# Fixed buffers for the z2 tiles of a gMLP kernel: which buffer each of the last two tiles takes

## The chip, the cores and the metric

The kernel runs on one core of a Trainium2 chip. The metric is the time of one execution in device microseconds; a kernel's time is the median of several runs. Five engines work beside each other and wait for one another through semaphores: PE (TensorE, matmuls), ACT (ScalarE), DVE (VectorE), POOL (GpSimd) and SP (SyncE). Each runs its own instructions in order. DMAs are issued from the queues of SP, ACT and POOL.

## The reference

One block: a layer norm with modulation, a long convolution (an S4 state space model), and then a gMLP, which is where the change lies:

```python
z = gelu(einsum("bsd,df->bsf", x, w_in))        # s = 2048 rows, f = 4608
z1 = z[..., :2304]
z2 = layernorm(z[..., 2304:], axis=-1)
g = einsum("ts,bsf->btf", w_sp, z2) + b_sp[None, :, None]
out = einsum("bsf,fd->bsd", z1 * g, w_out)
```

The layer norm of z2 needs a whole row of 2304 values, and g sums over all 2048 rows, so every row of z2 must be finished before the first g is complete.

## The kernel before

The first stage is the convolution (`ssm`, up to about 440 us). Then come two phases.

**Phase A** (`phase_a`, L1250) makes z2 in 16 tiles b of 128 rows x 2304. A tile is made in five blocks h: matmuls on PE (`z2_mm`, L1212), then a gelu on ACT from the bank into the tile's buffer (`z2_gelu`, L1219). DVE takes the statistics (`z2_stats`, L1227; `roots`, L1166); ACT normalizes the tile in place (`z2_norm`, L1236; for odd b in one operation, for even b in two, after DVE has subtracted the halves in `z2_diff`, L1231); POOL's queue stores the tile to DRAM in two halves (`z2_store`, L1245, tensor `z2_d`). All this stands in program order on each engine (the class `Pinned`). In the loop over b (L1339), tile b - 1 is normalized and stored while tile b is made: ACT's order there is the first gelu of tile b, the norm of tile b - 1, the second gelu of tile b. Beside it run the splitting of w_in and w_sp into two f16 parts (`wso`, `wsp`) and the norms of other weights.

A tile's buffer can be written again when both halves of the store that reads it have landed. The pool `zp` (L1256) has three buffers of 9,216 bytes per partition; they go round, so tile b stands in buffer b mod 3 and waits for the stores of tile b - 3. In the built program the buffers taken by tiles 0, 2 and 1 start at 132544, 141760 and 150976. So the last tiles stand as follows: tile 13 in the highest, tile 14 in the middle, tile 15 in the lowest.

**Phase B** (`phase_b`, L1548) works in four quarters q of 512 output rows and nine groups f of 256 columns. It needs

- z1: `z1_unit` (L1408) makes 128 columns of z1 for 512 rows with 14 matmuls (L1415) and one gelu on ACT (L1420). Two units share one z1 tile. Six units come ahead of the first group.
- z2 "sets": for each n of 36 (four per group f) SP reads 512 KB of z2 (`z2_load`, L1118, `raw<-z_d`, four buffers, on SP's queue in program order). The set n % 4 = 3 holds tiles 12 to 15. Set n is built (`z2_build`, L1121) from seven sums, each split into two f16 parts: DVE makes the sums (L1081 to L1083), ACT the upper parts (L1129), DVE the lower parts (L1130). There are three buffers of sets. In the first quarter the finished set is also stored from ACT's queue (L1444, `set_d<-zset`) for the quarters after.
- PE multiplies each set with w_sp in 2 x 7 x 3 = 42 matmuls (L1450 to L1452) into four banks per group; DVE adds up the banks (L1465, `gt`) and multiplies with z1, which is then overwritten with its two f16 parts for the product with w_out (`out_block`).

On PE, ACT and DVE a scheduler has set the order in phase B when the program was built; the queue of SP stays in program order. On ACT that order at the joint is: norm of tile 15, both gelus of the first z1 tile, first gelu of the second z1 tile, and then the builds of the first three sets.

The pool `bp` of phase B lies on memory that phase A has left. In the built program the first z1 tile lies at 109600, the second at 134176 to 138272, the third at 130080 to 134176, `gt` at 138272 to 142368, and two later z1 tiles at 142368 to 150560. The second z1 tile so lies inside the lowest z2 buffer, and nothing of `bp` lies in the highest. Whoever first writes such a tile waits for the stores of the z2 tile that lay there.

Of the kernel before, what the change touches and what calls it, by code (L numbers as in the profile page):

```python
# [9 lines left out]
F32 = mybir.dt.float32  # L10
# [12 lines left out]
FH = 2304  # L23
# [775 lines left out]
class Mlp:  # L799
# [419 lines left out]
    def z2_gelu(self, b, h):  # L1219
        n = min(512, FH - 512 * h)  # L1220
        if h == 0:
            self.zs[b] = self.zp.tile([128, FH], F32, name="z2")
            self.bz[b] = self.ap.tile([128, 6, 6], F32, name="bsz")
        self.nc.scalar.activation(self.zs[b][:, 512 * h:512 * h + n], self.pzs.pop((b, h))[:, :n], AF.Gelu_apprx_tanh,
                                  scale=self.wcol(5 + h, INV_IN))
# [24 lines left out]
    def phase_a(self):  # L1250
# [2 lines left out]
        cpa = ExitStack()  # L1253
        self.pa = self.pool(cpa, "pa", 6, space=PSUM)
        self.ps1 = lambda: self.pa.tile([128, 512], F32, name="pz")
        self.zp = self.pool(self.c2, "zp", 3)  # L1256
        self.wp = self.pool(self.ctx, "wp", 7, side="right")

        self.fp = self.pool(self.ctx, "fp", 1, side="right")
# [468 lines left out]
```

## Time and profile before

| | |
|---|---|
| time, median of 3 runs | 1784.21 us (1781.14 to 1785.44) |
| time of the profiled execution | 1783.02 us |
| its span, first to last instruction | 1781.2 us |
| mean granted TensorE clock | 0.98 |
| PE busy | 1693.0 us, 95% of the span |
| DVE busy | 1119.1 us, 63% |
| ACT busy | 785.2 us, 44% |
| POOL busy | 223.9 us, 13% |
| phase A, about | 440 to 685 us |
| first z1 product on PE | 674.88 us |

How to read it: the profile is one execution. All moments are us from the start of its span. A busy PE says only that matmuls are in flight; they overlap, so the start of one to the start of the next is the better measure. Time in which an engine other than PE idles costs something only if PE, or what PE waits for, waits in turn.

### The profile page before, as it was taken

The page shows a single profiled execution, that of the slowest core. Times are in us where ns is not written, and L with a number is a line of the kernel's source. Part 1 is how long each engine was busy: PE and PEld are TensorE (multiplying, and loading weights), DVE is VectorE, ACT ScalarE, POOL GpSimd, SP SyncE. Part 2 cuts the span into 40 slices and gives each one's busy share as a digit, 9 for nine tenths or more (in the row PEclk, how much of TensorE's full clock was granted, in tenths as well). Part 3 has the DMA queues.
Part 4 walks back from the last instruction along what each step waited for, and adds up shares of the span by engine and source line. Part 5 has one row for each costly group of instructions (what it writes and reads, how often), then busy time and mean ns, then how long its engine had stood idle before and what let it go on. Part 6 is the DMA issues. An engine that isn't in the chain of part 4 may idle for free.

```text
span 1781.2 us, 33976 instructions
## 1 busy us (share of the span) xinstructions
PE 1693.0 (95%) x14202; PEld 1195.6 (67%) x14202; DVE 1119.1 (63%) x2182; ACT 785.2 (44%) x1023; POOL 223.9 (13%) x350
## 2 busy tenths in 40 slices
PE   5688999997999999999999999999999999999999
PEld 1344555565545555877787777887778787787787
DVE  7988999858899996988783544483222274222322
ACT  5669999854576665555351322241211132011110
POOL 1321222342122110000000000000000000000000
PEclk8788999998999999999999999999999999999999
DMA  8457545799598887876654666562655572555520
GB/s 277 140 206 236 144 129 162 188 250 303 165 289 285 268 237 227 288 277 241 222 204 154 246 238 222 204 254 101 217 203 188 176 271 70 182 173 175 201 84 28
DMA packets 145866, 361.57 MB, mean 203 GB/s; under 512 B 23296, under 2 KB 59008, under 8 KB 143792
## 3 DMA queue, kind: packets, MB, share of 16 engines
q1 hardware_dynamic: 103104, 167.30, 29.7%
q0 software_dynamic: 33120, 153.95, 25.8%
q10 hardware_dynamic: 9488, 38.16, 5.3%
q8 instruction: 111, 1.82, 0.4%
q14 instruction: 43, 0.35, 0.1%
HBM read 256.86 MB, written 93.05 MB: 196 GB/s over the span
## 4 chain that ended last, share of the span: by engine, by line
PE 59%; DVE 10%; issue 6%; DMA 4%; ACT 3%; SPq 0%; POOL 0%; ACTq 0%; DVEq 0%; POOLq 0%
PE ps L1452 10%; PE ps L1450 10%; PE ps L1451 10%; PE ps L1415 9%; PE pz L132 5%; PE ps L1505 3%; PE ps L1502 3%; PE ps L1504 3%; PE pk L132 2%; DVE zset L1130 2%; ACT z L132 1%; DVE gt L1465 1%; DMA gbs<-in_w_out 1%; DVE bsz L132 1%; DMA zset<-set_d 1%
## 5 line engine op out<-in xcount | busy, mean ns | idle before, releaser
L1450 PE MATMUL ps<-wsp,zset 128*128 128x256 f16 x2016 | 549.5, 273 | 6.3 <-DVE gt L1465 3.7
L1452 PE MATMUL ps<-wsp,zset 128*128 128x256 f16 x2016 | 549.5, 273 | 3.5 <-DVE zset L1130 3.4
L1451 PE MATMUL ps<-wsp,zset 128*128 128x256 f16 x2016 | 549.5, 273 | 0.0
L132 PE MATMUL pz<-wz,nt 128*128 128x512 f16 (+1 forms) x1120 | 224.7, 361 | 4.7 <-ACT nt L132 4.7
L1465 DVE SCALAR_TENSOR_TENSOR gt<-ps,sc,bsp 128x512 f32<-128x512 f32 x33 | 24.8, 750 | 316.4 <-PE ps L1452 316.4
L1415 PE MATMUL ps<-n2q,wf 128*128 128x512 f16 x1008 | 223.1, 379 | 0.0
L1450 PEld LDWEIGHTS <-zset 128*128 128x128 f16 x2016 | 197.5, 98 | 33.3 <-DVE gt L1465 4.3
L1452 PEld LDWEIGHTS <-zset 128*128 128x128 f16 x2016 | 197.3, 98 | 27.8 <-DVE zset L1130 4.9
L1451 PEld LDWEIGHTS <-zset 128*128 128x128 f16 x2016 | 197.3, 98 | 25.9
L132 PEld LDWEIGHTS <-nt 128*128 128x128 f16 x1120 | 110.1, 99 | 110.9 <-ACT nt L132 5.5
L1415 PEld LDWEIGHTS <-wf 128*128 128x128 f16 x1008 | 98.6, 98 | 111.7
L1427 POOL DMA_DIRECT2D zset<-set_d x96 | 50.8, 529 | 973.8 <-PE ps L1452 960.9
L1420 ACT ACTIVATE z<-ps,sc 128x512 f32<-128x512 f32 x56 | 37.9, 681 | 284.6 <-PE ps L1415 274.9
L1504 PE MATMUL ps<-wout,z 128*128 128x288 f16 x448 | 127.6, 286 | 0.0
L1505 PE MATMUL ps<-wout,z 128*128 128x288 f16 x448 | 127.6, 286 | 0.0
L1502 PE MATMUL ps<-wout,z 128*128 128x288 f16 x448 | 126.0, 286 | 0.9 <-ACT ot L1512 0.9
L1465 DVE SCALAR_TENSOR_TENSOR gt<-ps,sc,gt 128x512 f32<-128x512 f32 (+1 forms) x165 | 112.1, 696 | 5.4
L1130 DVE TENSOR_TENSOR zset<-raw,zset 128x1024 f16<-128x1024 f32 x48 | 58.7, 1224 | 84.3 <-ACT zset L1129 84.3
L1129 ACT ACTIVATE zset<-raw 128x1024 f16<-128x1024 f32 x48 | 50.3, 1050 | 95.8 <-PE ps L1452 55.5
L1520 DVE TENSOR_TENSOR ot<-ot,ps 128x288 f32<-128x288 f32 x31 | 14.0, 453 | 78.3 <-ACT ot L1512 78.3
L369 PE MATMUL ps<-ln_x,r1t 128*128 128x288 f32 x128 | 42.6, 491 | 19.2 <-ACT kab L437 8.0
L1512 ACT ACTIVATE ot<-ps 128x288 f32<-128x288 f32 x32 | 12.8, 408 | 106.2 <-PE ps L1502 88.1
(356 smaller groups left out, 2864.0 us busy)
## 6 DMA issues: line engine op xcount, KB each, us to landing
zset<-set_d POOLq DMA_DIRECT2D x96, 896.0 KB, 4.9
set_d<-zset ACTq DMA_DIRECT2D x36, 896.0 KB, 5.9
raw<-z_d SPq DMA_DIRECT2D x48, 512.0 KB, 4.7
wf<-win_d SPq DMA_DIRECT2D x72, 320.0 KB, 3.5
raw<-in_w_spT SPq DMA_DIRECT2D x43, 512.0 KB, 6.1
z_d<-z POOLq DMA_DIRECT2D x32, 576.0 KB, 7.9
u_d<-st1o POOLq DMA_DIRECT2D x16, 576.0 KB, 4.4
u<-u_d SPq DMA_DIRECT2D x36, 256.0 KB, 4.6
```

Of the source, the lines that this page charges most:

```text
L132: return self.tc.keep_in_program_order(f(*a, **k))
L1129: nc.scalar.activation(o[:, k, 0], t, AF.Copy)
L1130: nc.vector.tensor_tensor(o[:, k, 1], t, o[:, k, 0], op=ALU.subtract)
L1415: nc.tensor.matmul(pm.rearrange("p (t c) -> p t c", t=4), w[:, kw], self.n2[q][:, :, kn], start=i == 0, stop=i == len(Z1) - 1)
L1427: self.nc.gpsimd.dma_start(o, self.set_d[n // 4, n % 4])
L1450: T.matmul(pm, z[:, a, 0, c], w[:, b, 0], start=i + half == 0, stop=False, skip_group_check=True)
L1451: T.matmul(pm, z[:, a, 0, c], w[:, b, 1], start=False, stop=False, skip_group_check=True)
L1452: T.matmul(pm, z[:, a, 1, c], w[:, b, 0], start=False, stop=i == 7, skip_group_check=True)
L1465: V.scalar_tensor_tensor(dst, pm, inv, to, op0=ALU.mult, op1=ALU.add)
L1502: T.matmul(pl, p[:, 1, ts], w[:, 0, hs], start=st, stop=sp)
L1504: T.matmul(pa, p[:, 0, ts], w[:, 0, hs], start=st, stop=False)
L1505: T.matmul(pa, p[:, 0, ts], w[:, 1, hs], start=False, stop=sp)
```

## The change

Each of the three buffers gets a name of its own, and the last two tiles choose theirs: tiles 0 to 13 take buffer b mod 3 as before, tile 14 takes buffer 0 and tile 15 buffer 2. The pool then holds one buffer for each of three names, and these are placed in the order in which they are first used.

```diff
@@ z2_gelu
         if h == 0:
-            self.zs[b] = self.zp.tile([128, FH], F32, name="z2")
+            self.zs[b] = self.zp.tile([128, FH], F32, name="z2%d" % (b % 3 if b < 14 else 2 * b - 28))
             self.bz[b] = self.ap.tile([128, 6, 6], F32, name="bsz")
@@ phase_a
-        self.zp = self.pool(self.c2, "zp", 3)
+        self.zp = self.pool(self.c2, "zp", 1)
```

In the built program buffers 0, 1 and 2 start at 132544, 141760 and 150976, so tile 13 stands in the middle buffer, tile 14 in the lowest, tile 15 in the highest. The instructions of all engines stand in the same order as before; what differs is which semaphores some of them wait for. DMASW is one of eight semaphores that POOL's stores use in turn.

On ACT in phase A, at tile 14's first gelu (z_6949; z_6802 is tile 13, wsst a weight whose norm is taken):

```order
 L132 ACTIVATE wsst,acc<-wsst 128x1024 [waits DMAHW1_49,Activation_49]
 L132 ACTIVATE wsst,acc<-wsst 128x1024 [waits DMAHW2_49,Activation_49]
-L132 ACTIVATE z_6949<-pz,sc 128x512 [waits DMASW1_49,DMASW0_49,PE_49]
+L132 ACTIVATE z_6949<-pz,sc 128x512 [waits DMASW3_49,DMASW4_49,PE_49,Activation_49]
 L132 ACTIVATE z_6802<-z_6802,nm_6972,r_6971 128x2304 [waits DVE_49,Activation_49]
 L132 ACTIVATE z_6949<-pz,sc 128x512 [waits PE_49]
```

The gelu waited for the two halves of tile 11's store (DMASW 0 and 1) and now waits for those of tile 12's (DMASW 3 and 4).

On ACT at the joint of the phases, at the gelus of the first z1 tile (z_7305), of the second (z_7338) and at the first build:

```order
 L1420 ACTIVATE z_7305<-ps,sc 128x512 [waits DMASW5_49,DMASW2_49,PE_49]
 L1420 ACTIVATE z_7305<-ps,sc 128x512 [waits PE_49]
-L1420 ACTIVATE z_7338<-ps,sc 128x512 [waits DMASW3_49,DMASW4_49,PE_49,Activation_49]
+L1420 ACTIVATE z_7338<-ps,sc 128x512 [waits DMASW2_49,DMASW1_49,PE_49]
 L1129 ACTIVATE zset<-raw 128x4x256 [waits DMAHW7_49,Pool_49]
 L1129 ACTIVATE zset<-sum 128x3x256 [waits DVE_49]
```

The second z1 tile waited for the two halves of tile 15's store (DMASW 3 and 4 again, one round later) and now waits for those of tile 14's (DMASW 1 and 2).

In the same way tile 15's first gelu waited for tile 12's store and now waits for tile 11's; the first write of `gt` waited for the stores of tiles 14 and 15 and now waits for those of tiles 13 and 14; the first late z1 tile waited for tile 14's and now waits for tile 13's. Tiles 1 and 2 have changed places, so that tile 1's first gelu now has the waits for what the convolution left in the middle buffer, which tile 2 had.

## The prediction

> **What bounds the kernel now.** PE is busy nearly all of the span (table above), so time can only come from places where PE waits. The change touches the last z2 tiles and the first z1 tiles, so I went to the chain that ended last around that joint.
>
> ```profile
> 682.26 2.32 ACT z L132
> ...
> 685.02 1.01 POOL z_d L132
> 686.04 6.84 DMA z_d<-z
> ```
>
> From 682 us the chain is not on PE: tile 15 is normalized, its store is issued, and the chain sits 6.84 us in the store's later half. ACT's timeline shows who waits for it, with the idle time ahead of a row and what ended it in brackets.
>
> ```profile
> 684.48 1.25 ACT L1420 ACTIVATE z<-ps,sc 128x512 f32<-128x512 f32 x2
> 692.99 0.69 ACT L1420 ACTIVATE z<-ps,sc 128x512 f32<-128x512 f32 x1 [7.26 <-DMA z_d<-z]
> ...
> 696.78 0.34 ACTq L1444 DMA_DIRECT2D set_d<-zset  x1
> ```
>
> The second z1 tile's first gelu waits 7.26 us for tile 15's store, and the builds of the first z2 sets (L1129) queue behind it on ACT. The last row is the store of the first set, which goes when the set is complete. DVE makes the lower half of each set (L1130) after ACT:
>
> ```profile
> 694.65 1.23 DVE L1130 TENSOR_TENSOR zset<-raw,zset 128x1024 f16<-128x1024 f32 x1 [11.35 <-ACT zset L1129]
> ...
> 705.27 0.43 DVE L1081 TENSOR_TENSOR sum<-raw 128x256 f32<-128x256 f32 x1
> ...
> 717.96 0.75 DVE L1465 SCALAR_TENSOR_TENSOR gt<-ps,sc,bsp 128x512 f32<-128x512 f32 x1
> ```
>
> PE, which multiplies the sets, in its timeline and, below, its waits between 673 and 735 us (us in total, times, longest):
>
> ```profile
> 674.88 18.29 PE L1415 MATMUL ps<-n2q,wf 128*128 128x512 f16 x84
> ...
> 696.92 0.27 PE L1450 MATMUL ps<-wsp,zset 128*128 128x256 f16 x1
> 697.03 0.27 PE L1451 MATMUL ps<-wsp,zset 128*128 128x256 f16 x1
> ...
> 707.42 0.28 PE L1452 MATMUL ps<-wsp,zset 128*128 128x256 f16 x1 [0.37 <-DVE zset L1130]
> ...
> 750.45 0.28 PE L1452 MATMUL ps<-wsp,zset 128*128 128x256 f16 x1 [1.31 <-DVE zset L1130]
> ```
>
> ```profile
> PE ps L1450 <- ACT zset L1129: 2.2, 1, 2.2
> PE ps L1452 <- DVE zset L1130: 2.1, 3, 1.0
> ```
>
> PE has z1 products until 674.88 + 18.29 = 693.17, so it feels only the tail of ACT's wait: 2.2 us, and then three waits for DVE, 2.1 us together, the last at 707.42. DVE started its builds late and only then has caught up; the wait at 750.45 is for DVE once more. Busy time by stretch (length; then busy us and instructions of PE, PEld, DVE, ACT, POOL; granted clock; DMA share; GB/s) says that DVE has nothing to spare here:
>
> ```profile
> 695.00:735.00 40.00, 37.49 (x339) 32.91 (x340) 39.12 (x62) 23.83 (x28) 0.00 (x0) 1.00 0.76 276
> ```
>
> **The change part by part.** No instruction moves on any engine; only buffers do, and with them waits. The landing times of the stores (issue to landing, the two halves of tile 12 and then of tile 14, each below its issue row) price them; tile 15's later half is the 6.84 us from 686.04 in the chain.
>
> ```profile
> L132 POOL DMA_DIRECT2D z_d<-z x2: 1007/1009/1011, 646.3 to 647.3; - x2
> DMA to landing us min/median/max: 5.4/7.0/8.6
> L132 POOL DMA_DIRECT2D z_d<-z x2: 1002/1004/1007, 673.5 to 674.5; - x2
> DMA to landing us min/median/max: 5.4/6.4/7.5
> ```
>
> *The wait that goes.* The second z1 tile now lies on tile 14's buffer. Tile 14's later half lands at 674.5 + 7.5 = 682.0; ACT is free at 684.48 + 1.25 = 685.7. The gelu starts there, 7.3 us earlier, with 3.7 us to spare. ACT's first builds follow at once (no wait of theirs is put down to a read), and so does DVE: its row at 694.65 moves to 687.4.
>
> *What PE makes of it.* PE is on z1 until 693.2 and then needs the first set complete (its store at 696.78, now 689.5). All four waits up to 707.42 go: 2.2 + 2.1 = 4.3 us as drawn. A matmul is drawn 0.27 us long but the next one starts 0.11 later (696.92, 697.03), so each wait hides another 0.16: 4 x 0.16 = 0.6. PE is **5.0 us** ahead, 4.9 to 5.0 by the rounding. It reaches the matmul of 707.42 at 702.4, while the half that it awaited there comes 7.3 us earlier, at 700.1: 2.3 us of cover.
>
> *What is late next.* PE, for DVE's sums of the first product group (717.96). Four sets of 42 matmuls at 0.11 from 693.0 end at 711.3 to 711.5, and the bank that DVE reads first closes six matmuls sooner, near 711. DVE could be there at 717.96 - 7.3 = 710.7, so it waits 0.3 to 0.6 us and stays about 6.8 us ahead. From there it works without a gap to the build that PE awaited at 750.45 for 1.31 + 0.16 = 1.47 us. With DVE 6.8 and PE 5.0 ahead that wait is gone: PE is 5.0 + 1.5 = **6.5 us** ahead. From below, if only the waits up to 707 went, it would be 5.0; from above, the whole 7.3. Nothing behind that is tied to a fixed moment: what PE waits for later was itself started by PE, ACT or DVE.
>
> *A read that cannot follow.* The fourth read of z2 holds tiles 12 to 15. It used to go when DVE freed its buffer; now it must wait for tile 15's store, which lands at 686.04 + 6.84 = 692.9:
>
> ```profile
> L132 SPq DMA_DIRECT2D raw<-z_d x1: 320/320/320, 695.9 to 695.9; - x1
> DMA to landing us min/median/max: 4.2/4.2/4.2
> ```
>
> It moves from 695.9 to 692.9, 3.0 us instead of 7.3, and on SP's queue the next z2 reads stand behind it. Landing at 697.1, it is in time for DVE's use of it (705.27 - 7.3 = 698.0) by 0.9 us. I take a cost of nothing. The bound from above is the slowest of all such reads from here on:
>
> ```profile
> DMA to landing us min/median/max: 3.3/4.6/9.5
> ```
>
> At 9.5 us it lands at 702.4, DVE loses 4.4 of its 7.3 us, and the gain is 2.9. It will see more traffic, too: the store of the first set, on ACT's queue, moves from 696.8 to 689.5, on top of tile 15's store. Packets of the two queues, tile 15's in 690 to 692 us and the set's in 698 to 700 us (packets, MB, share), the first stretches in which the one ends and the other begins:
>
> ```profile
> q0 software_dynamic: 85, 0.29, 55.5%
> q10 hardware_dynamic: 75, 0.54, 64.6%
> ```
>
> Tile 15's packets fill about half of 690 to 692; those of the set's store begin at 698, 1.2 us after its issue, so now at 690.7. [...]
>
> *The wait that comes.* Tile 14 now takes tile 12's buffer, one tile ago instead of tile 11's. ACT's rows there (tile 14's first gelu, tile 13's norm, tile 14's second gelu):
>
> ```profile
> 652.21 0.71 ACT L132 ACTIVATE z<-pz,sc 128x512 f32<-128x512 f32 x1
> 655.88 2.31 ACT L132 ACTIVATE z<-z,nm,r 128x2304 f32<-128x2304 f32 x1 [2.96 <-DVE nm L132]
> 658.09 0.67 ACT L132 ACTIVATE z<-pz,sc 128x512 f32<-128x512 f32 x1
> ```
>
> and DVE's statistics of tile 14:
>
> ```profile
> 659.95 1.01 DVE L132 BATCH_NORM_STATS2 bsz<-z 128x6 f32<-128x384 f32 x2
> ```
>
> Tile 12's later half lands at 647.3 + 8.6 = 655.9, so that gelu goes from 652.2 to 656.0. Behind it on ACT stands the norm of tile 13, which waited for DVE until 655.88 anyway; it starts near 656.7, 0.8 us late, and all behind it on ACT with it. DVE, on which the chain lies here, takes tile 14's first two gelus at 659.95, and the second now ends at 658.09 + 0.67 + 0.8 = 659.6: 0.3 us of cover. I take a cost of nothing; each us that the store lands later than 656.2 costs DVE one. The bound is the slowest of the 32 z2 stores (with three reads among the landings):
>
> ```profile
> DMA to landing us min/median/max: 5.3/7.7/13.9
> ```
>
> At 13.9 it lands at 661.2 and takes 5.0 us off the head start: gain 2.3. [...]
>
> *The rest.* Tile 15's gelu waits for tile 11's stores, older than tile 12's: nothing. The gate sums and the last z1 tiles wait for tiles 13 and 14, landed by 682.0: nothing. Tiles 1 and 2 swap buffers, which moves a wait for the last stores of x1 from tile 2 to tile 1; they were issued before tile 0 was computed, and no wait of either tile for them shows: nothing.
>
> **Sum.** 6.5 us from the profiled run of 1783.02 us (span 1781.2, 1.8 us around it) leaves 1776.5. The median of the runs, 1784.21, is 1.2 above that run: **1777.7 us**.
>
> **The rivals.**
> *The head start is cut.* The fourth read or tile 12's store lands late. DVE's lead is then 7.3 less the delay, and PE cannot be further ahead than DVE at 750. For it: 0.9 and 0.3 us of cover, against landings that spread by several us. Against it: the set's store meets only the last packets of tile 15's. [...]
> *Given back.* The lead survives to 750 and is lost where PE next depends on something that did not move, such as a read for the next quarter. For it: a DMA share of 0.76. Against it: reads are started by buffers coming free. Time: 1784.2.
> *Slower: the new wait replaces the old.* Same place on ACT, tile 14's first gelu, with everything behind it. Once tile 12's store lands after 656.2 + 7.3 = 663.5 (16 us after issue) the head start is used up, and PE, which needs that gelu's bank back for tile 15, stalls as well. At 20 us it lands at 667.3, 3.8 us past break-even: 1788.0. Against it: 13.9 is the longest landing seen.
> *It does not do what it says.* If the compiler placed the three names in another order, z1 would still wait for tile 15; but the waits in the order above name tile 14's stores. Part of "given back".
>
> **How the numbers follow.** About 0.3% (5.4 us) is what a measurement of this kernel can tell from no change. Forecast 0.62, head start cut 0.26, given back 0.08, slower 0.04. Runs spread from 1781.1 to 1785.4, so a forecast of 6.5 us shows as more than 5.4 in some five cases of six: 0.52; from the cut head start 0.05 more: faster 0.57. Same: 0.10 + 0.21 + 0.08 + 0.01 = 0.40. Slower 0.03. The range goes from the whole head start (7.3) with 2 us of spread below, 1775.0, to the slowest store, 1782.0; beyond lie given back, slower, and a little more.
>
> **What would show it.** In the profile after: ACT's row at L1420 near 685.7 without a wait; the first L1450 at 693.0 to 693.2 and no wait up to 711; tile 14's first gelu at 656.0; the fourth read at 692.9; no wait at 744 on PE (750.45 less 6.5); the same clock. Wrong if DVE waits at its first L1081 after that read, if DVE's statistics of tile 14 start after 660, or if PE waits in the later quarters grow.

## The result and the profile after

| | before | changed |
|---|---|---|
| median of 6 runs each | 1782.4 us (1781.1 to 1785.4) | 1772.9 us (1770.0 to 1776.4) |
| profiled execution: span | 1781.2 us | 1768.2 us |
| PE's first z1 instruction | 672.51 us | 668.23 us |
| from there to the end of the span | 1108.7 us | 1099.9 us |

The ratio is 0.994, 95% interval 0.9923 to 0.9956: 9.5 us between the medians, against the 6.5 that were forecast. 1772.9 us lies below the forecast's range (1775.0 to 1782.0). The forecast gain taken from this comparison's own 1782.4 would have been 1775.9; so of the 4.8 us by which the time was missed, 1.8 are the level of before, which six runs put lower than three had, and 3.0 are the gain.

PE's first z1 instruction is a semaphore instruction of line L1415 in PE's queue; the first z1 matmul starts 2.37 us behind it in every execution (at 674.88 and 670.61 here). The expectations below, where they count from "its first z1 matmul", count from this instruction.

The last two rows of the table split the profiled pair: it differs by 8.8 us behind that instruction and by 4.3 us ahead of it, in a stretch where the change only exchanges tiles 1 and 2 and adds one wait, at tile 14.

At the joint, ACT's timeline (start, us, engine, line, operation) shows the step that was forecast. Three z1 gelus stand in one row without idle time, the builds behind them:

```profile
680.34 1.82 ACT L1420 ACTIVATE z<-ps,sc 128x512 f32<-128x512 f32 x3
682.05 1.06 ACT L1129 ACTIVATE zset<-raw 128x1024 f16<-128x1024 f32 x1
...
685.26 0.35 ACTq L1444 DMA_DIRECT2D set_d<-zset  x1
```

DVE's first build, two of its sums that wait for reads, and its first sum of the product group:

```profile
683.14 1.22 DVE L1130 TENSOR_TENSOR zset<-raw,zset 128x1024 f16<-128x1024 f32 x1 [3.94 <-ACT zset L1129]
...
696.20 0.42 DVE L1081 TENSOR_TENSOR sum<-raw 128x256 f32<-128x256 f32 x1 [0.36 <-DMA raw<-z_d]
...
699.68 0.42 DVE L1081 TENSOR_TENSOR sum<-raw 128x256 f32<-128x256 f32 x1 [0.26 <-DMA raw<-z_d]
...
706.76 0.75 DVE L1465 SCALAR_TENSOR_TENSOR gt<-ps,sc,bsp 128x512 f32<-128x512 f32 x1
```

Then all of PE's waits between 690 and 1110 us, of the changed kernel and then of before (us in total, times, longest):

```profile
PE ps L1450 <- DVE gt L1465: 1.9, 2, 1.7
PE ps L1502 <- ACT ot L1512: 0.7, 1, 0.7
PE ps L1450 <- DMA zset<-set_d: 0.3, 1, 0.3
```

```profile
PE ps L1450 <- DVE gt L1465: 3.7, 2, 2.4
PE ps L1452 <- DVE zset L1130: 3.4, 4, 1.3
PE ps L1450 <- ACT zset L1129: 2.2, 1, 2.2
PE ps L1502 <- ACT ot L1512: 0.9, 1, 0.9
PE ps L1450 <- DMA zset<-set_d: 0.3, 1, 0.3
```

The two groups on which the forecast was built (<- ACT zset, <- DVE zset) are gone. A third one, the waits for DVE's sums, has shrunk from 3.7 to 1.9. The prediction does not have these rows of before:

```profile
787.74 0.28 PE L1450 MATMUL ps<-wsp,zset 128*128 128x256 f16 x1 [1.34 <-DVE gt L1465]
...
863.42 0.28 PE L1450 MATMUL ps<-wsp,zset 128*128 128x256 f16 x1 [2.36 <-DVE gt L1465]
```

In the changed kernel the first wait is down to 0.22 us and the second to 1.71:

```profile
775.55 0.28 PE L1450 MATMUL ps<-wsp,zset 128*128 128x256 f16 x1 [0.22 <-DVE gt L1465]
...
850.58 0.28 PE L1450 MATMUL ps<-wsp,zset 128*128 128x256 f16 x1 [1.71 <-DVE gt L1465]
```

### The profile page after: what moved, and what is told of

Read it like the earlier page. It is cut to its first block, busy times and chain, and to the rows that moved or that the text cites. A ratio compares the mean times of both kernels' runs of the same rounds, so it can differ in the third digit from the quotient of the medians.

```text
span 1768.2 us, 33975 instructions
## 1 busy us (share of the span) xinstructions
PE 1689.0 (96%) x14202; PEld 1193.5 (67%) x14202; DVE 1118.1 (63%) x2182; ACT 785.0 (44%) x1023; POOL 223.8 (13%) x350
## 4 chain that ended last, share of the span: by engine, by line
PE 55%; DVE 12%; issue 7%; DMA 5%; ACT 3%; POOL 0%; SPq 0%; ACTq 0%; DVEq 0%; POOLq 0%
PE ps L1450 10%; PE ps L1452 10%; PE ps L1451 10%; PE ps L1415 9%; PE pz L132 4%; PE ps L1504 3%; PE ps L1505 3%; PE ps L1502 3%; DVE zset L1130 2%; DVE gt L1465 1%; PE pk L132 1%; DVE bsz L132 1%; ACT z L132 1%; DMA gbs<-in_w_out 1%; DMA zset<-set_d 1%
## 5 line engine op out<-in xcount | busy, mean ns | idle before, releaser
L1450 PE MATMUL ps<-wsp,zset 128*128 128x256 f16 x2016 | 549.5, 273 | 2.2 <-DVE gt L1465 1.9
L1415 PE MATMUL ps<-n2q,wf 128*128 128x512 f16 x1008 | 223.1, 379 | 0.0
L1450 PEld LDWEIGHTS <-zset 128*128 128x128 f16 x2016 | 197.5, 98 | 29.2 <-DVE gt L1465 2.5
L1415 PEld LDWEIGHTS <-wf 128*128 128x128 f16 x1008 | 98.6, 98 | 111.7
L1512 ACT ACTIVATE ot<-ps 128x288 f32<-128x288 f32 x32 | 12.7, 407 | 106.8 <-PE ps L1502 88.6
```

Of the source, the lines that this page charges most:

```text
L1415: nc.tensor.matmul(pm.rearrange("p (t c) -> p t c", t=4), w[:, kw], self.n2[q][:, :, kn], start=i == 0, stop=i == len(Z1) - 1)
L1450: T.matmul(pm, z[:, a, 0, c], w[:, b, 0], start=i + half == 0, stop=False, skip_group_check=True)
```

## How the runs are compared

Set n begins on PE with the weights of L1450's matmul number 14n + 1, which are loaded 0.1 to 0.2 us ahead of the matmul, in the same order in every kernel here. The time from PE's first z1 instruction to that load leaves out what came ahead of the joint. Set 4 lies just behind the joint, set 12 behind the wait of 750 us, set 18 behind the one of 787, set 36 (the second quarter) behind the one of 863. The table holds all profiled executions, those of the experiments below too, but for e5 and e6, in which PE waits inside the z1 products; the first six have the old place of tile 15, in the lowest buffer.

| execution | set 4 | set 12 | set 18 | set 36 | end | DVE's waits for z2 reads, 690 to 720 us | stores of tile 0 to tile 11 |
|---|---|---|---|---|---|---|---|
| before, first | 43.8 | 88.1 | 123.3 | 292.8 | 1108.7 | 0 | 157.7 |
| before again (e7) | 44.7 | 88.8 | 123.9 | 295.1 | 1111.3 | 0 | 157.8 |
| before third (e14) | 44.1 | 88.3 | 122.9 | 290.4 | 1106.2 | 0 | 157.4 |
| names (e1) | 44.4 | 88.9 | 123.4 | 294.9 | 1110.6 | 0 | 157.2 |
| names again (e13) | 44.5 | 89.0 | 124.6 | 295.7 | 1111.9 | 0 | 157.5 |
| before, read moved (e10) | 44.5 | 89.1 | 123.4 | 295.5 | 1111.4 | 0 | 157.6 |
| changed, first | 38.7 | 81.4 | 115.4 | 284.1 | 1099.9 | 0.6 | 156.2 |
| changed again (e4) | 38.9 | 84.0 | 117.6 | 288.0 | 1103.8 | 2.5 | 159.2 |
| changed third (e8) | 38.7 | 82.6 | 116.7 | 289.3 | 1105.0 | 1.3 | 160.2 |
| changed fourth (e12) | 38.8 | 81.8 | 116.8 | 288.3 | 1103.9 | 0.6 | 160.0 |
| changed fifth (e15) | 38.7 | 82.9 | 116.9 | 287.7 | 1103.6 | 1.5 | 160.4 |
| changed, read moved (e9) | 38.7 | 81.7 | 116.3 | 288.3 | 1104.6 | 0.5 | 159.0 |
| rotation (e2) | 39.1 | 84.8 | 119.4 | 287.9 | 1103.6 | 3.5 | 158.1 |
| rotation again (e11) | 38.7 | 81.9 | 117.7 | 287.3 | 1104.1 | 0.9 | 159.0 |
| two buffers (e3) | 39.2 | 82.0 | 116.6 | 287.6 | 1104.9 | 0.8 | 168.0 |

## The experiments

Theory J: the wait for tile 15's store at the joint is the whole effect, and what the first pair differs by ahead of the joint is chance. Rivals: S (the exchange of tiles 1 and 2 helps), N (tile 14's new wait costs a part of the gain). After the first four runs a theory R was added: reads of z2 cut the head start in some executions; its rival C calls that spread without a cause here.

**e1 and e13: names without the moved tiles.** Tile 15 lies in the lowest buffer again.

```diff
-name="z2%d" % (b % 3 if b < 14 else 2 * b - 28)
+name="z2%d" % (b % 3)
```

> Names for the buffers, but all tiles go round (tile 15 in the lowest buffer on the second z1 tile, tile 14 in the highest); tiles 1 and 2 stand as in the changed kernel. Theory J (the joint is the whole effect, and the 4 us by which the changed kernel's profile is ahead before 640 us are chance of the early stages): ACT's second z1 gelu waits about 7 us for tile 15's store again, PE's four waits between 690 and 711 us are back, time as before, 1780 to 1784. Theory S (the exchanged tiles 1 and 2 make phase A faster): 3 to 4 us faster than before, about 1778.5, with no more than 3.4 us of PE wait near 498 us.

> Names alone again (all tiles go round). Up to tile 13 its program is that of the changed kernel, word for word. Theory J: time as before within 0.15%; PE reaches set 36 some 294 to 295.5 us after its first z1 matmul; tile 6 of phase A takes anywhere from 13 to 18 us, as in every kernel. If tile 6 takes 15.4 to 15.8 again while the changed kernel in this call takes 17 or more, something other than the program text sets it, and that stays open.

Measured: 1786.8 us against 1788.3 of before beside it, ratio 0.9989 (0.9969 to 1.0008); and 1786.3 against 1786.9, ratio 0.9988 (0.9969 to 1.0007). The wait on ACT is back (e1):

```profile
697.28 0.69 ACT L1420 ACTIVATE z<-ps,sc 128x512 f32<-128x512 f32 x1 [7.42 <-DMA z_d<-z]
```

and so are PE's waits, 690 to 900 us (e1):

```profile
PE ps L1450 <- DVE gt L1465: 3.5, 2, 2.8
PE ps L1450 <- ACT zset L1129: 2.8, 1, 2.8
PE ps L1452 <- DVE zset L1130: 2.5, 3, 1.3
```

The level of before is some 5 us higher in the experiments than in the first comparison, so only kernels measured beside each other are set against each other. Both intervals reach down to 0.9969, which is 5.5 us, so alone they do not rule out the 3 to 4 us of S. But phase A has none of it: the exchange shortens the step to tile 2's store by 0.2 us, and from tile 0's first store to tile 15's last it takes 212.4 and 212.6 us, in the three executions of before 212.3 to 213.0. Set 12 comes as late as in before. The gain comes with tile 15's place.

**e2 and e11: no short wait.** The buffers go round without exception from the highest; tile 13 is lowest, 14 in the middle, 15 highest.

```diff
         self.zp = self.pool(self.c2, "zp", 1)
+        for i in range(3):
+            self.zp.tile([128, FH], F32, name="z2%d" % i)
...
-name="z2%d" % (b % 3 if b < 14 else 2 * b - 28)
+name="z2%d" % ((b + 2) % 3)
```

> The three buffers go round without exception, but tile 0 starts in the highest, so that tile 13 stands in the lowest, tile 14 in the middle, tile 15 in the highest. No tile waits for the store of the tile two before it, and the second z1 tile waits for tile 13's store. Theory J (the wait for tile 12's store is covered): as the changed kernel, 1771 to 1775, no wait at tile 14's first gelu, everything at the joint as in the changed kernel. Rival N (the new wait of tile 14 costs a part of what it hides): 0.3 to 1 us faster than the changed kernel. If tile 0 should wait for what the convolution left in the highest buffer, it shows at 443 us and costs its length.

> The placement by rotation from the highest buffer once more, beside the changed kernel on the same chip. Theory J (the short wait of tile 14 costs nothing): within 1 us of the changed kernel, 5 to 9 us faster than before; the first comparison's lead over the changed kernel (0.9944 against 0.9968 of before) was spread. Rival N (the short wait costs): again 2 us or more faster than the changed kernel.

Measured: ratios 0.9944 (0.9923 to 0.9965) and 0.9964 (0.9948 to 0.9979); the changed kernel had 0.9968 and 0.9972 beside them. Tile 14 has no wait here. The stretch from tile 11's store to tile 15's is 54.1 and 54.0 us, and 53.8 to 54.3 in the changed kernel's five executions, 53.7 to 54.3 in those of before: the short wait costs nothing that shows there. N finds no support in that stretch; the small lead of the rotation is within the intervals, so it is at best an equal version. The second z1 tile and the joint are as in the changed kernel.

**e3: two buffers.** Now 14 tiles wait for the tile two before.

```diff
-name="z2%d" % (b % 3 if b < 14 else 2 * b - 28)
+name="z2%d" % (b % 2)
```

> Only two buffers: every tile from the third on waits at its first gelu for the store of the tile two before it, 14 times the wait that tile 14 has in the changed kernel (4.1 us on ACT there); tile 14 in the lower, tile 15 in the upper buffer, the joint as in the changed kernel. Theory J (the wait is covered by the norm's own wait for DVE, cover 0.1 to 0.3 us): no more than 0.2 us each, 1773 to 1776. Rival N (stores land late often enough to use the cover up): each us that a store lands after the cover's end delays DVE and then PE, about 0.5 us a tile, 1780.

Measured: 1788.2 us, ratio 0.9998 (0.9978 to 1.0017): all of the gain is lost. The changed kernel beside it (e4) had 1782.7, 5.5 us less. ACT's waits in phase A (us in total, rows, longest):

```profile
ACT z L132 <- DMA z_d<-z: 55.7, 13, 7.1
```

From tile 0's store to tile 11's it takes 168.0 us instead of 157 to 160, while from 11 to 15, where tile 14's wait lies, it takes 54.4: as ever. Four steps are 2 to 3.5 us longer than in before's first profile: to tile 1's store, to tile 2's, to tile 5's and to tile 8's. So both theories were half right: the wait is covered at tile 14, as theory J and the prediction had it, and J was wrong to carry that cover over to every tile; N had the price about right, but as 0.5 us at each tile, and it lies in four steps. Behind the joint e3 is a changed kernel like the others.

**e4, e8, e12, e15: the changed kernel again.**

> The changed kernel once more, for a second profile of it. Theory J: 1770 to 1776; at the last z2 store the profile is anywhere from 0 to 4 us ahead of that of before (in the first profile 4.1), with the half-clock stretches of the first 510 us elsewhere than in the first profile; from there to the end of the first quarter it gains about 9 us against before, as the first profile did, of it 7 at the joint. Theory S: again 4 us ahead by the last z2 store.

> The changed kernel a third time, on the chip of the last two kernels. Theory R: where DVE waits 0.4 us or less for each z2 read between 690 and 720 us, the stretch from tile 15's last store issue to the end is some 9 us shorter than in before; where it waits 2 to 3 us, some 5.5 us shorter. Rival C: the two do not go together.

> The changed kernel beside the kernels of this call. Theory J: ratio to before between 0.995 and 0.997; from the first z1 matmul to set 18 the gain is 8.0 us less what DVE waits beyond 0.6 us for its z2 reads (four executions so far: waits of 0.6, 1.3, 2.5 us gave 8.0, 7.1, 6.3). Rival C: no such relation.

> The changed kernel a fifth time. Theory J: set 36 at 284 to 289.3 us after the first z1 matmul, set 12 at 81.3 to 84, a mean gain of about 7 us behind the joint; ratio to before 0.995 to 0.9975. If the first comparison's 0.994 is the usual one, this run comes below 0.9955.

Measured: ratios 0.9968 (0.9955 to 0.9981), 0.9973 (0.9955 to 0.9991), 0.9972 (0.9958 to 0.9986), 0.9967 (0.9948 to 0.9987): 4.8 to 5.9 us. None reaches the first comparison's 9.5. In e4 two of DVE's sums wait for reads, 0.58 us and the 1.92 of the row below, and PE, which in the first profile had no wait left for DVE's builds, waits for them again (690 to 900 us):

```profile
708.57 0.42 DVE L1081 TENSOR_TENSOR sum<-raw 128x256 f32<-128x256 f32 x1 [1.92 <-DMA raw<-z_d]
```

```profile
PE ps L1452 <- DVE zset L1130: 2.0, 3, 1.3
PE ps L1450 <- DVE gt L1465: 3.2, 1, 3.2
```

The chain of waits (start, us, what) tells which read the longer one is for: one issued at 700.15, the fifth, right behind the fourth of 699.72 on SP's queue.

```profile
700.15 8.32 DMA raw<-z_d
```

This is the first rival of the prediction: PE's gain at set 12 is 88.7 - 84.0 = 4.7 us here, against the mean of the old placement. Read the table's sixth column against set 12: waits of 0.5 to 0.9 us go with 81.4 to 82.0 us, 1.3 with 82.6, 1.5 with 82.9, 2.5 with 84.0, 3.5 with 84.8. Each us that DVE waits for a read beyond the first half costs PE about one at set 12. That is a relation in nine executions, and e9 tries its cause.

**e9 and e10: the read without its wait.** Set 3 reads tiles 8 to 11 instead of 12 to 15, so it leaves out the last four tiles; sizes and order stay.

```diff
-self.z2_d[n // 4, n % 4].rearrange(
+self.z2_d[n // 4, 2 if n == 3 else n % 4].rearrange(
```

> The changed kernel, but the fourth read of z2 (set 3) takes tiles 8 to 11 again instead of 12 to 15, so that it does not wait for tile 15's store; the set holds the wrong tiles, all sizes and orders are as before. Theory R: the fourth read goes about 5 us earlier and no longer in a bunch with the fifth, DVE waits less than 0.3 us for a read between 690 and 720 us, PE gains 8 us or more from its first z1 matmul to set 18 (115.5 us or less, before 123.3 to 123.9) in this execution as in the best one of the changed kernel; 1 to 2 us faster than the changed kernel on the same chip. Rival C: set 18 after 116 to 119 us as in the other executions of the changed kernel, time the same.

> The kernel before with the same other address of the fourth read. Both theories: no change, since the read waited for its buffer there and not for the store: set 18 at 123 to 124 us after the first z1 matmul, time within 0.1% of before. If it is faster by more, the read costs something in before too and theory R's account of the changed kernel is too simple.

Measured: in the changed kernel 0.9956 (0.9935 to 0.9977), beside 0.9972 of e12; in before 0.9994 (0.9978 to 1.001), no change, as expected. SP's reads in e9 and DVE's only wait for one:

```profile
695.94 14.62 SPq L132 DMA_DIRECT2D raw<-z_d  x5
```

```profile
707.86 0.43 DVE L1081 TENSOR_TENSOR sum<-raw 128x256 f32<-128x256 f32 x1 [0.46 <-DMA raw<-z_d]
```

The fourth read goes 16.5 us after PE's first z1 instruction instead of 21.4 to 21.9, and the fifth behind it at 19.5 instead of 21.8 to 22.4. e9's chain of waits has the fifth:

```profile
698.99 8.78 DMA raw<-z_d
```

It landed later after its issue than in e4 (8.32), and yet DVE waits only 0.46 us, because it went out some 2.5 us sooner. So the head start is cut by the fourth read, which waits for tile 15's store, and by the fifth, which stands behind it on SP's queue; that much of R holds, by this one execution. Its word "bunch" does not: 3 us apart from the fourth, the fifth landed no faster. Set 18 was due at 115.5 us or less and came at 116.3, no better than the best of the unmoved executions (115.4), and the time gained on e12 is not resolved by the two intervals; so what the late reads cost in time is not shown.

**e5 and e6: tile 15's store on another queue.**

```diff
-            self.nc.gpsimd.dma_start(self.z2_d[...
+            (self.nc.scalar if b == 15 else self.nc.gpsimd).dma_start(self.z2_d[...
```

> The changed kernel, with both halves of tile 15's store on ACT's queue right after the norm instead of POOL's; nothing else moves on any engine. Theory R (in some executions the reads of z2 that tile 15's store holds back until 7.7 us after its last issue go in a bunch with the next two, land 6 to 9 us later, and so cut DVE's head start): the store lands 2 to 3 us earlier, the fourth read goes earlier by as much, DVE does not wait for a read between 690 and 720 us, and PE's gain from the first z1 matmul to the end of the first quarter is 8 to 9 us; 2 to 3 us faster than the changed kernel on the same chip. Rival C (the difference between 5.5 and 8.9 us of gain is spread of the chip that has nothing to do with these reads): as the changed kernel within 1 us, gain again anywhere from 5 to 9.

> The kernel before, with tile 15's store on ACT's queue: a part of the change's effect without its placement. Theory J: ACT's second z1 gelu waits 2 to 3 us less for tile 15's store (4.3 to 5.3 instead of 7.3), DVE starts its builds as much earlier, PE's wait of 2.2 us for the first set goes, the wait at the joint shrinks in proportion; 2 to 3.5 us faster than before. Rival (only whole waits count, PE is held by DVE further on): no more than 1 us.

Measured: 1.0005 (0.9989 to 1.0021) and 0.999 (0.9975 to 1.0005): the whole gain is gone from the changed kernel, and before gains nothing that shows. The trace of e5, PE and SP's queue:

```profile
700.66 5.19 PE L1415 MATMUL ps<-n2q,wf 128*128 128x512 f16 x14 [5.81 <-DMA wf<-win_d]
```

```profile
682.79 14.42 SPq L132 DMA_DIRECT2D wf<-win_d  x3
697.51 1.95 SPq L132 DMA_DIRECT2D raw<-z_d  x2
```

PE now waits in the z1 products themselves, for weights. SP issues three reads of wf in 14.4 us; in the changed kernel's first profile the same three took 6.4:

```profile
673.82 6.36 SPq L132 DMA_DIRECT2D wf<-win_d  x3
```

In the built program the DMAs of SP's and ACT's queues take eight semaphores in turn (DMAHW0 to 7), and with two more of them the third wf read got the semaphore of one of tile 15's halves: it waits for DMAHW0 at 464, the value that this half of the store, issued from 689.74 on, brings it to, and goes out at 696.9. The experiment was meant for the reads of z2 and hit another read: it says nothing about R. For J it says a little: in e6 ACT's wait is 4.77 us instead of 7.3, but PE's stall on wf hides what that gave.

**e7 and e14: before again.**

> The kernel before once more, for a second profile. Theory J: from tile 15's last store issue to the end 1094 to 1098 us (1095.2 in the first profile), all waits at the joint as in the first, while the moment of that issue itself lies anywhere from 682 to 692 us. Rival S2 (before is slower ahead of the joint for a reason of its own): that moment is again 686 or later and changed kernels stay below it.

> The kernel before a third time. Theory J: set 36 at 292.8 to 295.5 us after the first z1 matmul; the spread is that of the wait near 865 us and of a half-clock stretch behind it. Tile 6 anywhere from 13 to 18 us.

Measured: one run of 1786.8 us; and 0.9995 (0.9971 to 1.0019). The three executions of before end 1106.2 to 1111.3 us behind PE's first z1 instruction. Most of that spread arises between sets 28 and 30, which take 9.8 to 14.7 us in the six executions with the old placement and 10.8 to 14.8 in the others.

## Why the forecast was right, and where it failed

*The wait that goes: right.* The second z1 tile's gelu does not wait. DVE's first build starts at 683.14; put on before's time by the 4.28 us that separate PE's first z1 instructions, that is 687.4, the moment forecast. In the repeats nothing of ACT's wait comes back.

*What PE makes of it: right.* 5.0 us at 707 were forecast. At set 4 the first pair gives 43.76 - 38.73 = 5.0; the five executions of the changed kernel against the six with the old placement give 5.6 on average. In five of those six PE's first wait is longer than the 2.2 us of the first profile (2.3 to 2.9), and a half-clock stretch of 3.41 us lies at the joint as well, which no execution of the changed kernel has there (last section). The prediction put "the same clock", which holds for the first pair only.

*DVE, and the wait at 750: right in the first pair, an upper case otherwise.* DVE was to be 6.8 ahead at its first sum of the group: 717.96 became 706.76, less 4.28 is 6.9. At set 12, 6.5 were forecast; the first pair has 6.8, and the five executions average 82.5 against 88.7, which is 6.2, between 4.7 and 7.3.

*The read that cannot follow: the step was right, its price was not nothing.* The fourth read went at 689.63 (row below), 693.9 on before's time, 1.0 later than forecast.

```profile
689.63 2.36 SPq L132 DMA_DIRECT2D raw<-z_d  x3
```

The prediction named the reads that stand behind it on SP's queue and then priced only the fourth. In this execution the fourth came in time, and DVE's wait at 696.20 is for the fifth:

```profile
690.06 6.05 DMA raw<-z_d
```

The wait at 699.68 is for the sixth. Over the five executions DVE waited 0.6 to 2.5 us for these reads together, where 0.9 us of cover and no cost had been put. In the four repeats the fourth itself was late, by 0.6 to 1.5 us, and that is one of the prediction's own signs of being wrong (a wait at DVE's first L1081 after that read). That the set's store, moved beside tile 15's, would cost nothing was the author's estimate. Tile 15's later half, with the set's store issued at 685.26 beside it (in 685 to 690 us their queues' packets fill 39.7% and 49.4%), landed at 689.37, 7.5 us after its issue at 681.9 where 6.84 stood in before; that is 693.65 on before's time and 0.8 us late. How much of this is due to the store beside it, no run shows.

*The wait that comes: right.* Tile 14's first gelu, and DVE's statistics of that tile:

```profile
652.20 0.69 ACT L132 ACTIVATE z<-pz,sc 128x512 f32<-128x512 f32 x1 [4.13 <-DMA z_d<-z]
```

```profile
655.94 1.01 DVE L132 BATCH_NORM_STATS2 bsz<-z 128x6 f32<-128x384 f32 x2
```

655.94 + 4.28 = 660.2, where 659.95 stood in before: 0.3 us late and just beyond the 660 that the prediction named as a sign, and the next stores make it up (tile 11 to 15 above). e2 takes the wait away and gains nothing in that stretch.

*The step that failed* is the sum's end: "6.5 us ahead", "from above, the whole 7.3", and "Nothing behind that is tied to a fixed moment". The working stopped at 750 and took DVE's head start as a cap. Two more waits for DVE lay behind it in before (787.74 and 863.42 above). In the first pair PE's lead grew to 7.9 at set 18 and to 8.7 at set 36, 1.9 us past set 12 and above the cap. The cap itself did not hold: DVE's lead at its first sum of a product group is 6.9 us in the first three groups of that pair and then 7.7, 7.6 and 8.8; where DVE gained the rest is not shown. In the repeats the same stretch gave and took: set 12 to set 36 takes 202.1 to 206.7 us in the old placement and 202.7 to 206.7 in the new, on average 205.4 and 204.9. So it is worth 0.5 us in the mean, with a spread of some 2 us to each side, and the range had no term for it. The range's "2 us of spread below" was too little, too: the spread of the stretch ahead of the joint (last section) comes on top.

Taken over all executions, the part behind PE's first z1 instruction is 1110.0 us long with the old placement (six) and 1103.2 in the changed kernel (five): 6.8 us, or 5.9 by the four repeats alone. That this is so near the sum of 6.5 is in part luck: the joint gave 5.6 where 5.0 stood, the wait of 750 gave 0.6 where 1.5 stood, and the stretch behind gave 0.5 where nothing stood. What the first comparison measured was more, in the four repeats it was less. That the first pair's 8.8 us is a favourable draw of the reads and of the stretch from set 12 to set 36 is shown by the repeats. The 9.5 us of its medians are not reproduced by any of the four (the rotation, equal at the joint, had 0.9944 once and 0.9964 once), and whether the chip of that comparison or chance made it, the runs do not say; the cause of those 3 us beyond the forecast stays open.

The rivals: *the head start is cut* happened in part: 4.7 us of gain at set 12 in e4, 3.9 in the rotation's first execution, both above the 2.9 and 2.3 that the prediction worked out for the slowest read and the slowest store. *Given back* did not happen: the lead of set 36 is still there at the end. *Slower* did not: the longest of the five waits at tile 14 seen was 4.4 us.

## What to carry to other kernels

Follow a head start through every later wait of the critical engine until none is left, not only to where it first meets one; each may add to it or take from it. A cover found at one tile holds for that tile: the same wait that cost nothing at tile 14 cost 5.5 us by the medians when it came at every tile. Where the gain is half a per cent, compare several profiled executions from a common moment inside the kernel: 6.8 us stood out behind the joint, while ahead of it executions of one program, the changed kernel, differed by up to 9.6 (668.23 and 677.85).

## What was not expected of the hardware

*Half-clock stretches behind short waits.* The changed kernel's first profile has none behind 440 us; before has one of 6.83 us at 500 (stretch, length, busy time of PE, PEld, DVE, ACT and POOL, granted clock, DMA share, GB/s; before, then changed):

```profile
500.00:508.00 8.00, 6.92 (x19) 2.58 (x20) 6.91 (x20) 6.68 (x13) 2.74 (x4) 0.57 0.99 318
```

```profile
500.00:508.00 8.00, 8.00 (x41) 3.98 (x40) 7.46 (x24) 6.14 (x11) 1.47 (x3) 1.00 0.98 334
```

PE's waits just ahead of that are alike, and only once did the clock fall (before, then changed):

```profile
501.08 9.11 PE L132 MATMUL pz<-wz,nt 128*128 128x512 f16 x28 [3.66 <-ACT nt L132]
```

```profile
498.07 6.22 PE L132 MATMUL pz<-wz,nt 128*128 128x512 f16 x28 [3.42 <-ACT nt L132]
```

The 28 matmuls take 9.11 us and 6.22. Near 865 us, too, some of PE's waits for DVE's sums go with such a stretch. In e8 it was 4.1 us long, until 861.37, and the clock fell at 860.62:

```profile
858.00:870.00 12.00, 8.63 (x68) 7.27 (x69) 11.34 (x19) 3.65 (x5) 0.00 (x0) 0.86 0.61 244
```

In e15 a wait of 2.26 us had such a stretch, in e4 one of 3.25 had none. With such a stretch sets 28 to 30 take 13.4 to 14.8 us, without it 9.8 to 12.7. At the joint the old placement has one in five of six executions, behind PE's waits for the sets; the changed kernel has none there (e7, then changed):

```profile
697.00:703.00 6.00, 4.66 (x26) 3.32 (x27) 6.00 (x11) 3.84 (x5) 0.00 (x0) 0.72 0.66 236
```

```profile
690.00:696.00 6.00, 6.00 (x57) 5.37 (x56) 5.81 (x10) 3.84 (x6) 0.00 (x0) 1.00 0.93 270
```

In the clock events of the first pair's two traces all of them are one or more times 3.41 us long (3.41 to 17.07), but for the last, which the end cuts. The 0.86 of e8's 12 us and the 0.72 of e7's 6 us are each what one stretch of 3.41 us at half clock gives. What sets its length, and why waits of like length end differently, no run shows.

*Equal programs, different times.* Up to tile 13 names and the changed kernel are one program. Yet the step to tile 6's store took 14.8 to 15.8 us in five executions with the old placement outside the first comparison, and 17.2 to 18.5 in five with the new one, e9 included; in the first pair it was 13.6 and 12.9. The placement does not settle it: e6, with the old one, took 17.5, the rotation 16.2 and 17.1, and e3 12.5. ACT waits there for reads of w_out, 525 to 580 us (in total, times, longest), in e15 and in e13:

```profile
ACT wsst L132 <- DMA wsst<-in_w_out: 6.1, 3, 4.0
```

```profile
ACT wsst L132 <- DMA wsst<-in_w_out: 1.9, 1, 1.9
```

In the profiled executions this takes some 2 us off the changed kernel's 6.8, and it may be why the later comparisons come out near 5; that is not shown, since only the profiled executions can be split. What makes the reads land later there is open.
